# Agent attention with a cosine feed-forward on one core: lots of scores put right behind two kinds of exponential bursts, and the bursts eight steps later

## The chip, the cores and the metric

The kernel runs on one core of one Trainium2 chip. The time is the device time of one execution in microseconds, from a median of three runs. The core has a matrix engine (TensorE, PE in the profile, with its weight loads as PEld), a vector engine (VectorE, DVE), a scalar engine (ScalarE, ACT), GpSimd (POOL) and the engine whose queue starts the transfers (SyncE, SP). Each takes its own instructions in order and waits for the others by semaphores. PE writes only into the banks of PSUM, from which DVE and ACT read.

## The reference

Four batches of 12480 tokens, 128 channels, 49 agents. The agents attend to the keys, the queries attend to the agents, and the result goes token by token through a feed-forward layer with 2048 hidden units and the activation h cos h.

```python
def _attn_ref(q, k, v, agents):
    scale = 1.0 / np.sqrt(q.shape[-1])
    def sm(a, b):
        s = scale * (a @ b.transpose(0, 2, 1))
        s = s - s.max(-1, keepdims=True)
        e = np.exp(s)
        return e / (e.sum(-1, keepdims=True) + 1e-09)
    a2k = sm(agents, k)
    agent_v = a2k @ v
    q2a = sm(q, agents)
    return (q2a @ agent_v).astype(np.float32)

def _moe_ref(x, w_in, w_out):
    h = x @ w_in
    g = h * np.cos(h)
    return (g @ w_out).astype(np.float32)
```

## The kernel before

The tokens of a batch are cut into 13 groups of 960, so there are 52 groups in all. After a prologue, in which the agents of batch 0 are finished and the weights are unpacked, one main loop runs over 832 steps, 16 per group (two halves of 480 tokens, eight pairs of hidden blocks). A step (lines 535 to 572) makes two matmuls of the hidden layer into a double bank `ph` (L543), a sine on ACT (L546, `c`), a product on DVE (L548, `r`), and, four steps later, two matmuls of the output layer into a bank `one` (L565). There are three double banks `ph` and two single banks `one`. One of the two `one` banks holds the sum of the output layer for eight steps; then ACT copies it out (L567, `osb`). So all other uses of `one` share the other bank, one after another.

Between these steps the loop works ahead for later groups and batches. The pieces of this extra work are:

- a **query lot** (`query`, L334 to 351): a tile of 960 queries is loaded (`xt`, three buffers), multiplied with the agents (L92, eight matmuls in the program, sixteen in the trace, into `one`), then DVE takes the maximum of each token (L343, `mx`) and subtracts it (L350, `e`), which sets the bank free;
- a **key lot** (`Agents.scores`, L158 to 182): the same matmuls for 960 keys, then ACT copies the bank out (L171, `s`) and DVE keeps a running maximum (L180 for the first, L182);
- a **burst**: the exponentials of four or five key lots (L214) and of four or five query lots (L354) stand together on ACT, with a table load ahead of and behind them. DVE then sums the query weights and inverts the sums (L358 to 360). Each batch has three bursts, and one earlier burst, of queries 3 to 7, stands at the start of the loop;
- the **maximum** of a batch's keys (`top`, `across`, `spread`) and its subtraction on POOL (L210), which must be over before the first burst;
- the **values** lots (L233), the sums of the exponentials on POOL (L222), and the projection of the new agents into the weights `a` (L264 to 272);
- for each group the weights on POOL (L364) and their transposition (`query_turned`: four matmuls L373, a copy L375 on ACT, casts L378 and L379 on POOL into `pT`).

The places are set by a table of steps made ahead of the loop. `extra` (L451) gives a piece that needs the bank `one` the next free step of those whose place in the run of eight allows it (1, 3, 5; with `dense` 1 to 5). `spread_out` (L464) spreads a list of pieces evenly up to a given step. `BURSTS` (L393) holds the steps of a batch's three bursts, counted from the batch's start. The table fixes in which order the program issues its instructions; the framework then still moves instructions of one engine past each other by estimates of its own, except for the exponentials, which are kept in place. So where a lot's eight matmuls really stand between the `ph` and `one` matmuls is seen only in the built program.

Of the kernel before, what the change touches and what calls it, by code (L numbers as in the profile page):

```python
# [40 lines left out]
def agent_attention_cos_ffn(ctx, tc, qT, kT, v, agT, w_in, w_out, outT):  # L41
    nc = tc.nc
# [108 lines left out]
    class Agents:  # L151
# [3 lines left out]
        def __init__(self, sb, psum, b, wide=None):  # L155
            self.sb, self.psum, self.b, self.wide = sb, psum, b, wide

        def scores(self, g):  # L158
            sb = self.sb
            if g == 0:  # L160
                self.s = sb.tile([TT, NT, NA], F32, name="s", bufs=1)
                self.run = sb.tile([TT, GT, NA], F32, name="run", bufs=1)

                av = sb.tile([P, 2 * HI], F32, name="av", bufs=2)
                self.av, self.sums = av[:, :KR], self.copies(av)
                nc.gpsimd.memset(av[:, NA:HI], 0.0)
                self.es = sb.tile([TT, GT, NA], F32, name="es", bufs=1)
            src = kT[self.b, :, g * GRP:(g + 1) * GRP]
            s = self.part(g)
            if self.wide is None:  # L170
                nc.scalar.copy(s, scores(sb, src, self.b, self.psum()))  # L171
            else:
                if g % 2:
                    xt = sb.tile([P, 2, CH], F32, name="c", bufs=3).rearrange("p j x -> p (j x)")
                else:
                    xt = sb.tile([P, GRP], F32, name="xt", bufs=3)
                ps = scores_twice(xt, src, self.b, self.wide())
                nc.scalar.copy(s.rearrange("p (h t) a -> p h t a", h=2), ps)
            if g == 0:
                nc.vector.tensor_copy(self.run, s)  # L180
            else:
                nc.vector.tensor_max(self.run, self.run, s)  # L182
# [117 lines left out]
    with ExitStack() as pools:  # L300
# [89 lines left out]


        assert NG == 13
        BURSTS = (100, 124, 148)  # L393
        first, early = (0, 1, 2), (3, 4, 5, 6, 7)
        pieces = [tuple(tuple(range(b * NG + x, min(b * NG + y, NQ))) for x, y in ((8, 12), (12, 16), (16, 21))
                        if b * NG + x < NQ) for b in range(NB)]
# [67 lines left out]
        def spread_out(todo, t, end):  # L464

            for i, lot in enumerate(todo):
                t = extra(t, *lot) + 1
                if i + 1 < len(todo):
                    t += max(0, (end - t) // (len(todo) - i - 1) - 1)
            return t  # L470
# [6 lines left out]
        def scored(piece):  # L477
            return [(query, n, piece) for n in piece]

        t = spread_out(scored(early), 0, 0) + 2  # L480
        burst(t, early)
        for b in range(1, NB):
            o, ps = (b - 1) * PER, pieces[b - 1]
            qs, ks = scored(ps[0]), [(ab[b].scores, g) for g in range(NG)]
            if b > 1:
                qs += scored(ps[1])
            both = []
# [10 lines left out]

            for k, at in enumerate(BURSTS):
                at += o  # L500
                for g, n in lots[k:k + 1]:
                    plan(at, pinned_exp, ab[b], g, n)
                burst(at, ps[k])
                for g in range(*((lots[k - 1][0], sum(lots[k - 1])) if k else (0, 0))):
                    plan(at, ab[b].add, g)
                    extra(at, ab[b].values, g, dense=True)
                t = at + (6 if k else 1)
                if k == 0:
                    todo = scored(ps[2]) if b > 1 else scored(ps[1])
                elif k == 1:  # L510
                    todo = [] if b > 1 else scored(ps[2])
                else:
                    todo = []
                    for g in range(lots[2][0], NG):
                        plan(t, ab[b].add, g)
                        t = extra(t, ab[b].values, g) + 2
                t = spread_out(todo, t, o + BURSTS[min(k + 1, 2)] - 4)
# [195 lines left out]
```

## Time and profile before

| what | value |
|---|---|
| median of three runs | 1276.65 us (1271.73 to 1281.36) |
| the profiled execution | 1280.7 us, span 1278.9 us |
| PE busy | 1191.8 us, 93% |
| DVE busy | 1094.8 us, 86% |
| ACT busy | 1029.5 us, 80% |
| POOL busy | 315.2 us, 25% |
| granted PE clock, mean | 0.974 |
| first products (L548) | 83.4 us after the span's start |
| last products | end at 1271.6 us |

The main loop takes 1188 us of the span. A row of a group gives line, engine, operation, tiles and shapes, the number of instructions, then busy time and the mean of one, and the idle time of the engine ahead of them with what ended it. A row of the timeline gives start, length, engine, line, operation, how many were merged, and in brackets the idle time before and what ended it. A row of the windows gives a stretch of time, its length, the busy time of each engine with the number of its instructions, the granted PE clock (1.00 is full speed, 0.50 half) and the share and rate of the transfers.

### The profile page before, as it was taken

How to read it: one execution, taken by the hardware profiler on the slowest of the kernel's cores; microseconds unless marked ns; L12 is line 12 of the kernel's file. 1: busy time of each engine (PE TensorE's matmuls, PEld its weight loads, DVE VectorE, ACT ScalarE, POOL GpSimd, SP SyncE). 2: the span in 40 equal slices, each digit the busy share in tenths (PEclk: the TensorE clock that was granted, in tenths of full speed). 3: DMA queues.
4: the chain of work that ended last, by engine and by line, in shares of the span. 5: the costliest groups of instructions: out<-in, count | busy, mean ns of one | idle time of the engine just before them, and what ended most of it. 6: DMA issues, size and time to landing. Idle time of an engine off the chain costs nothing.

```text
span 1278.9 us, 17272 instructions
## 1 busy us (share of the span) xinstructions
PE 1191.8 (93%) x6349; PEld 961.8 (75%) x6349; DVE 1094.8 (86%) x1217; ACT 1029.5 (80%) x1130; POOL 315.2 (25%) x341
## 2 busy tenths in 40 slices
PE   8998999899999999989999999998999999989997
PEld 8977888687877777768787777777788776667664
DVE  6778888878898888888889888888888999989997
ACT  2357887887798878787979878878888999889997
POOL 1202111621231211162222212224421222121220
PEclk9788999899999999989999999998999999999999
DMA  8762233033412223214231223222320010000000
GB/s 308 223 190 78 77 111 122 32 110 114 135 45 93 77 78 108 78 47 124 78 109 58 66 82 104 77 77 76 95 93 32 31 47 31 16 31 16 32 32 34
DMA packets 39189, 107.74 MB, mean 84 GB/s; under 512 B 4344, under 2 KB 4728, under 8 KB 39096
## 3 DMA queue, kind: packets, MB, share of 16 engines
q1 hardware_dynamic: 39096, 106.55, 26.1%
q8 instruction: 52, 0.85, 0.3%
q14 instruction: 41, 0.34, 0.1%
HBM read 80.97 MB, written 25.56 MB: 83 GB/s over the span
## 4 chain that ended last, share of the span: by engine, by line
PE 57%; DVE 20%; ACT 14%; issue 7%; POOL 1%; DMA 0%; ACTq 0%; SPq 0%; DVEq 0%; POOLq 0%
PE ph L543 20%; DVE r L548 15%; PE one L565 13%; PE one L92 11%; ACT c L546 9%; PE one L233 5%; ACT osb L567 3%; PE ph L233 2%; PE one L561 1%; DVE mx L343 1%; PE one L264 1%; PE ph L100 1%; DVE run L182 1%; PE one L562 1%; ACT e L354 1%
## 5 line engine op out<-in xcount | busy, mean ns | idle before, releaser
L548 DVE SCALAR_TENSOR_TENSOR r<-c,ph 128x960 fp32r<-128x960 f32 x832 | 924.5, 1148 | 108.0 <-ACT c L546 104.1
L546 ACT ACTIVATE c<-ph,half_pi 128x960 f32<-128x960 f32 x832 | 863.2, 1066 | 165.5 <-PE ph L543 145.6
L543 PE MATMUL ph<-pT,a 113*128 113x480 f32 x1664 | 549.6, 411 | 53.9 <-DVE r L548 52.2
L565 PE MATMUL one<-r,w 128*128 128x480 f32 x1664 | 518.0, 391 | 3.8 <-ACT osb L567 3.3
L543 PEld LDWEIGHTS ph<-pT,a 113*128 113x128 f32 x1664 | 285.5, 192 | 178.4 <-DVE r L548 88.5
L565 PEld LDWEIGHTS one<-r,w 128*128 128x128 f32 x1664 | 313.0, 192 | 52.0 <-ACT osb L567 6.4
L364 POOL TENSOR_TENSOR p<-e,rz 120x392 f32<-120x392 f32 x52 | 44.2, 854 | 644.6 <-PE one L373 573.6
L92 PEld LDWEIGHTS one<-ag,xt 128*120 128x120 f32 x1408 | 167.0, 186 | 31.4 <-ACT osb L567 24.1
L92 PE MATMUL one<-ag,xt 128*120 128x49 f32 x1408 | 167.3, 266 | 8.0 <-ACT osb L567 7.0
L379 POOL TENSOR_TENSOR pT<-p,pT 49x480 fp32r<-49x480 f32 x104 | 127.0, 1221 | 7.9
L378 POOL CAST pT<-p 49x480 fp32r<-49x480 f32 x104 | 63.3, 609 | 160.9 <-ACT p L375 156.4
L233 PEld LDWEIGHTS one<-s,vt 120*128 120x128 f32 x624 | 76.5, 191 | 8.2 <-DVE av L238 2.6
L233 PE MATMUL one<-s,vt 120*128 120x98 f32 x624 | 78.2, 273 | 1.1 <-ACT osb L567 0.6
L567 ACT COPY osb<-one 128x480 f32<-128x480 f32 x104 | 57.5, 553 | 2.2 <-PE one L565 2.1
L222 POOL TENSOR_TENSOR es<-es,s 120x392 f32<-120x392 f32 x36 | 36.7, 1019 | 52.3 <-ACT s L214 49.9
L373 PEld LDWEIGHTS one<-ident,p 120*113 120x113 f32 x208 | 30.9, 181 | 16.2 <-ACT osb L567 12.0
L373 PE MATMUL one<-ident,p 120*113 120x120 f32 x208 | 37.4, 279 | 4.4 <-ACT osb L567 3.8
L561 PE MATMUL one<-pT,b 113*128 113x480 f32 x104 | 40.1, 386 | 0.0
L562 PE MATMUL one<-pT,b 113*128 113x480 f32 x104 | 39.7, 382 | 0.0
L375 ACT COPY p<-one 113x480 f32<-113x480 f32 x52 | 28.9, 556 | 12.2 <-PE one L373 12.2
L343 DVE TENSOR_REDUCE mx<-one 120x8 f32<-120x392 f32 x49 | 27.5, 561 | 13.1 <-PE one L92 13.1
L182 DVE TENSOR_TENSOR run<-run,s 120x392 f32<-120x392 f32 x48 | 31.4, 654 | 4.8 <-ACT s L171 2.4
(91 smaller groups left out, 520.3 us busy)
## 6 DMA issues: line engine op xcount, KB each, us to landing
xt<-qT SPq DMA_DIRECT2D x52, 480.0 KB, 3.5
vt<-v SPq DMA_DIRECT2D x104, 240.0 KB, 3.3
outT<-osb SPq DMA_DIRECT2D x51, 480.0 KB, 2.6
xt<-kT SPq DMA_DIRECT2D x46, 480.0 KB, 3.5
c<-kT SPq DMA_DIRECT2D x6, 480.0 KB, 5.9
raw<-w_in SPq DMA_DIRECT2D x8, 256.0 KB, 5.0
raw<-w_out SPq DMA_DIRECT2D x8, 256.0 KB, 4.3
outT<-osb SPq DMA_DIRECT2D x2, 240.0 KB, 2.8
```

The lines of the kernel that those rows point to most:

```text
L92: nc.tensor.matmul(ps[:, t, :], xt[:, t * TT:(t + 1) * TT], ag[:, b, :], start=True, stop=True)
L233: nc.tensor.matmul(po, vt[:, t, :], twice(e[:, t, :]), start=(t == 0 and (g == 0 or not lone)), stop=(t == GT - 1 and (g == NG - 1 or not ...
L373: nc.tensor.transpose(pt[:KR, t * TT:(t + 1) * TT], p_in[n % 2][:, t, :KR], ident[:TT, :TT])
L378: nc.gpsimd.tensor_copy(pT[own, c], p[own])
L379: nc.gpsimd.tensor_sub(pT[other, c], p[own], pT[own, c].bitcast(F32))
L543: nc.tensor.matmul(ph[:, j, :CH], ai[:, f], pTs[q % 3][:, c], start=True, stop=True)
L546: nc.scalar.activation(cos, h, AF.Sin, bias=half_pi, scale=1.0)
L548: nc.vector.scalar_tensor_tensor(r, cos, 1.0, h, op0=ALU.subtract, op1=ALU.mult)
L561: nc.tensor.matmul(po, b1[k], pTs[q % 3][:, c], start=False, stop=False)
L562: nc.tensor.matmul(po, b2[k], pTs[q % 3][:, c], start=False, stop=False)
L565: nc.tensor.matmul(po, w1[:, f, :], r[:, j, :], start=(f == 0), stop=(f == NF - 1))
L567: nc.scalar.copy(osb[:, c * CH:(c + 1) * CH], po)
```

## The change

Three things change in the table of steps, and one in how a key lot is copied.

- The three bursts of each batch stand at steps 108, 132 and 156 of the batch instead of 100, 124 and 148.
- The first three query lots that follow a batch's first burst (queries 12, 13, 14 in batch 1, 29 to 31 in batch 2, 42 to 44 in batch 3) get the next three consecutive steps behind the burst. Before, the first of them got the step behind the burst and the others were spread out.
- The first three key lots of batch 1 get consecutive steps (21, 22, 23) behind the early burst. Before, they stood at steps 21, 29 and 37.
- These three key lots are copied out of PSUM by DVE instead of ACT. All other key lots stay with ACT.

```diff
-        def scores(self, g):
+        def scores(self, g, by_vector=False):
...
-                nc.scalar.copy(s, scores(sb, src, self.b, self.psum()))
+                ps = scores(sb, src, self.b, self.psum())
+                if by_vector:
+                    nc.vector.tensor_copy(s, ps)
+                else:
+                    nc.scalar.copy(s, ps)
...
-        BURSTS = (100, 124, 148)
+        BURSTS = (108, 132, 156)
...
+        def beside(at, todo):
+
+            for lot in todo[:3]:
+                extra(at, *lot, dense=True)
+            return todo[3:]
+
         t = spread_out(scored(early), 0, 0) + 2
         burst(t, early)
+        beside(t, [(ab[1].scores, g, True) for g in range(3)])
+        t += 6
         for b in range(1, NB):
             o, ps = (b - 1) * PER, pieces[b - 1]
-            qs, ks = scored(ps[0]), [(ab[b].scores, g) for g in range(NG)]
+            qs, ks = scored(ps[0]), [(ab[b].scores, g) for g in range(3 if b == 1 else 0, NG)]
...
-                t = at + (6 if k else 1)
+                t = at + 6
                 if k == 0:
-                    todo = scored(ps[2]) if b > 1 else scored(ps[1])
+                    todo = beside(at, scored(ps[2]) if b > 1 else scored(ps[1]))
```

In the changed kernel all lines from 171 on have higher numbers: the hidden layer's matmuls are L555, the sine L558, the product L560, the output layer's matmuls L577, the maximum and the subtraction of a query lot L347 and L354, DVE's copy of a key lot L173.

How the built program's instructions stand is shown at three places. The first is PE at batch 2's first burst (step 308 before, 316 after). Here `ph` is the hidden layer, `r` the output layer, `ag,xt` a lot of scores, `p_94` the transposition of weights. Before, from the last `ph` ahead of the burst's wait on:

```order
L543 MATMUL ph<-pT_89,a_83 128x480 x2
L565 MATMUL one<-r,w_70 128x480 x2
L543 MATMUL ph<-pT_89,a_83 128x480 x2
L565 MATMUL one<-r,w_70 128x480 x2
L373 MATMUL one<-ident,p_94 113x120 x4
L543 MATMUL ph<-pT_89,a_83 128x480 x4
L565 MATMUL one<-r,w_70 128x480 x2
```

The same place after the change:

```order
L555 MATMUL ph<-pT_89,a_83 128x480 x2
L577 MATMUL one<-r,w_70 128x480 x2
L555 MATMUL ph<-pT_89,a_83 128x480 x2
L577 MATMUL one<-r,w_70 128x480 x2
L92 MATMUL one<-ag,xt 120x49 x16
L555 MATMUL ph<-pT_90,a_83 128x480 x2
L577 MATMUL one<-r,w_70 128x480 x2
```

Two whole lots now stand where the four transpositions stood, ahead of the next `ph`.

DVE at the same burst, before; `mx` and `e<-one,mx` are a query lot, `rz` the sums behind the exponentials, `r<-c,ph` the products of the steps:

```order
L548 SCALAR_TENSOR_TENSOR r<-c,ph 128x960 x5
L343 TENSOR_REDUCE mx_4927<-one 120x8
L350 TENSOR_TENSOR e<-one,mx_4927 120x392
L358 TENSOR_REDUCE rz_3577<-e 120x32
L359 TENSOR_SCALAR rz_3577<-rz_3577 120x32
L360 RECIPROCAL rz_3577<-rz_3577 120x32
L548 SCALAR_TENSOR_TENSOR r<-c,ph 128x960 x9
```

And after:

```order
L560 SCALAR_TENSOR_TENSOR r<-c,ph 128x960 x7
L347 TENSOR_REDUCE mx_5015<-one 120x8
L354 TENSOR_TENSOR e<-one,mx_5015 120x392
L347 TENSOR_REDUCE mx_5040<-one 120x8
L362 TENSOR_REDUCE rz_3655<-e 120x32
L354 TENSOR_TENSOR e<-one,mx_5040 120x392
L363 TENSOR_SCALAR rz_3655<-rz_3655 120x32
L560 SCALAR_TENSOR_TENSOR r<-c,ph 128x960
L364 RECIPROCAL rz_3655<-rz_3655 120x32
L560 SCALAR_TENSOR_TENSOR r<-c,ph 128x960 x2
L347 TENSOR_REDUCE mx_5063<-one 120x8
L560 SCALAR_TENSOR_TENSOR r<-c,ph 128x960
```

The second lot's two operations stand around the sums' reduction, and the third lot's behind the third product after the burst.

The third place is PE between the bursts, in batch 2, at the key lot that the table puts at step 225 (b_85 is a part of the projection of the output). Before, all eight of its matmuls stand between the two output matmuls of one step:

```order
L543 MATMUL ph<-pT_90,a_83 128x480 x2
L565 MATMUL one<-r,w_70 128x480
L92 MATMUL one<-ag,xt 120x49 x8
L565 MATMUL one<-r,w_70 128x480
L561 MATMUL one<-pT_89,b_85 128x480
L543 MATMUL ph<-pT_90,a_83 128x480 x2
```

After:

```order
L555 MATMUL ph<-pT_89,a_83 128x480 x2
L577 MATMUL one<-r,w_70 128x480 x2
L92 MATMUL one<-ag,xt 120x49 x3
L555 MATMUL ph<-pT_89,a_83 128x480 x2
L577 MATMUL one<-r,w_70 128x480 x2
L92 MATMUL one<-ag,xt 120x49 x3
L555 MATMUL ph<-pT_90,a_83 128x480 x2
L92 MATMUL one<-ag,xt 120x49 x2
L577 MATMUL one<-r,w_70 128x480 x2
```

The lot is cut into 3, 3 and 2 matmuls over three steps. The other two lots of the sixteen steps stand over two steps each (1 and 7 before, 2 and 6 or 1 and 7 after). At the early burst PE's order is the same up to step 21; two more lots then stand around the second output matmul of step 22, ahead of the `ph` of step 23.

## The prediction

> **What bounds the kernel now.** First the page: one core, 832 steps of the main loop, and three engines that are nearly full.
>
> ```profile
> span 1278.9 us, 17272 instructions
> PE 1191.8 (93%) x6349; PEld 961.8 (75%) x6349; DVE 1094.8 (86%) x1217; ACT 1029.5 (80%) x1130; POOL 315.2 (25%) x341
> ```
>
> No share says what a change is worth; the view by groups gives the parts of a step, and of a lot of scores (a lot is one 960-column tile of q or k).
>
> ```profile
> L548 DVE SCALAR_TENSOR_TENSOR r<-c,ph 128x960 fp32r<-128x960 f32 x832 | 924.5, 1148 | 108.0 <-ACT c L546 104.1
> L546 ACT ACTIVATE c<-ph,half_pi 128x960 f32<-128x960 f32 x832 | 863.2, 1066 | 165.5 <-PE ph L543 145.6 <-DVE r L548 4.3 <-issue 2.3
> ...
> L171 ACT COPY s<-one 120x392 f32<-120x392 f32 x39 | 19.0, 486 | 18.8 <-PE one L92 18.8
> ...
> L180 DVE COPY run<-s 120x392 f32<-120x392 f32 x4 | 1.4, 360 | 1.0 <-ACT s L171 1.0
> ```
>
> Sine and product follow one another at about 1.06 us, so ACT and DVE set a plain step. Where ACT waits, it waits for `ph`, that is for PE. Stretches of the loop show when (windows; columns: length, busy time of PE, PEld, DVE, ACT, POOL, then the granted clock). The first three are 16 steps each by the products (L548) counted in the timeline: one without lots, one with three in batch 2, one with three in batch 1. The last three are the 24 steps from each batch's first burst to its second.
>
> ```profile
> 1162.60:1180.80 18.20, 17.23 (x74) 12.33 (x73) 17.42 (x17) 17.49 (x20) 4.38 (x5) 1.00 0.07 28
> 455.40:478.60 23.20, 21.78 (x123) 17.83 (x122) 19.97 (x22) 18.82 (x22) 4.67 (x5) 1.00 0.27 85
> 156.80:178.90 22.10, 21.21 (x123) 17.98 (x122) 19.60 (x20) 18.79 (x21) 4.44 (x5) 1.00 0.28 91
> 237.70:276.90 39.20, 33.50 (x168) 26.83 (x167) 33.09 (x35) 32.27 (x33) 15.71 (x15) 0.91 0.21 64
> 554.40:595.20 40.80, 34.90 (x185) 29.03 (x183) 33.93 (x37) 32.25 (x34) 15.68 (x15) 0.92 0.25 73
> 863.30:903.30 40.00, 34.07 (x184) 28.39 (x183) 33.83 (x37) 32.10 (x34) 15.70 (x15) 0.91 0.25 75
> ```
>
> A plain step is 18.2/16 = 1.14 us. Three lots add 23.2 - 18.2 = 5.0 us in batch 2 and 3.9 us in batch 1: 1.67 and 1.30 us a lot, because a lot stands in PE's queue ahead of the next `ph`. I use 1.5. With lots the bound is PE, and a lot moved to where PE idles anyway is worth about that. Such a place is the burst; this is the timeline of batch 2's first one.
>
> ```profile
> 554.35 1.28 ACT L214 ACT_TABLE_LOAD   x1
> ...
> 555.43 0.56 DVE L343 TENSOR_REDUCE mx<-one 120x8 f32<-120x392 f32 x1
> 555.64 1.52 ACT L214 ACTIVATE s<-s 120x1568 f32<-120x1568 f32 x1
> ...
> 556.09 0.57 DVE L350 TENSOR_TENSOR e<-one,mx 120x392 f32<-120x392 f32 x1
> ...
> 557.06 1.50 ACT L354 ACTIVATE e<-e 120x1568 f32<-120x1568 f32 x1
> 557.19 0.57 PE L373 MATMUL one<-ident,p 120*113 120x120 f32 x4
> 558.57 1.28 ACT L546 ACT_TABLE_LOAD   x1
> 558.59 1.78 DVE L358 TENSOR_REDUCE rz<-e 120x32 f32<-120x1568 f32 x1 [1.93 <-ACT e L354]
> ...
> 560.41 0.79 DVE L359 TENSOR_SCALAR rz<-rz 120x32 f32<-120x32 f32 x1
> 561.24 0.35 DVE L360 RECIPROCAL rz<-rz 120x32 f32<-120x32 f32 x1
> 561.51 3.22 DVE L548 SCALAR_TENSOR_TENSOR r<-c,ph 128x960 fp32r<-128x960 f32 x3
> ...
> 562.75 2.13 PE L543 MATMUL ph<-pT,a 113*128 113x480 f32 x4 [4.98 <-DVE r L548]
> ...
> 565.48 1.00 PE L543 MATMUL ph<-pT,a 113*128 113x480 f32 x2
> ...
> 567.08 1.00 PE L543 MATMUL ph<-pT,a 113*128 113x480 f32 x2
> ...
> 570.33 1.78 PE L92 MATMUL one<-ag,xt 128*120 128x49 f32 x16
> ```
>
> For 5.5 us ACT makes no sine: table, two exponentials, table. PE fills three `ph` and then idles 4.98 us; DVE idles 1.93 us and then does the sums. PE comes back slow: its `ph` of two consecutive steps, 565.48 and 567.08, lie 1.60 us apart. The last row is the price of a lot on PE, 1.78 us.
>
> **Part by part: the first burst of each batch.** Two more query lots go in here, behind the one that stands ahead of the burst already. Count from the table load (554.35 = 0). The second lot takes PE where the transposes stood, 2.84, for 1.78: 4.62. DVE reduces it (0.56: 5.18), then, by its new order, the sums' reduction (1.78: 6.96, it began at 4.24 before), then subtracts (0.57: 7.53), scales (0.79: 8.3). The first product stands at 8.3; it was 7.16. The third lot waits for the one free bank of `one` until 7.53, ends at 9.3 with a full clock, and only then comes the next `ph`. DVE is the later one: products of three steps and the reciprocal to 11.8, the third lot's reduction 12.4, a product 13.4, its subtraction 14.0. So five steps take 14.0, nineteen plain ones 19 x 1.14 = 21.6, and the lots that stay outside 1.5 each: two in batches 2 and 3, one in batch 1. That makes 38.6, 38.6 and 37.1 against 40.8, 40.0 and 39.2: gains of 2.2, 1.4 and 2.1, mean 1.9. The loads are no limit: `xt` has three buffers, and those of the three lots are free before the burst.
>
> But PE still idles from 4.62 to 7.53, 2.9 us. The rows on the clock, in the windows and the timeline:
>
> ```profile
> 117.90:121.30 3.40, 1.29 (x6) 0.76 (x4) 2.89 (x3) 3.37 (x4) 0.00 (x0) 1.00 0.33 128
> 121.30:128.10 6.80, 6.14 (x17) 5.28 (x18) 5.48 (x7) 5.31 (x7) 4.00 (x5) 0.50 0.00 0
> 561.60:568.40 6.80, 5.65 (x14) 4.42 (x15) 6.13 (x6) 5.08 (x7) 6.51 (x8) 0.50 0.00 1
> ```
>
> ```profile
> 118.38 2.20 DVE L358 TENSOR_REDUCE rz<-e 120x40 f32<-120x1960 f32 x1 [1.43 <-ACT e L354]
> ...
> 121.96 1.17 PE L543 MATMUL ph<-pT,a 113*128 113x480 f32 x2 [2.77 <-DVE r L548]
> ```
>
> At the early burst an idle time of 2.77 us, 2.1 of it inside the 3.4 us before the change, was enough for 6.8 us at 0.50. So I take the half clock as likelier in the new gap too. It costs 0.6 us at the fifth step (the third lot takes 3.6 instead of 1.8, of which DVE's own lateness hides most) and then two steps at the 1.60 above instead of 1.14, about 1.4 together. Forecast per burst: 1.9 - 1.4 = 0.5 gained, 1.5 for three. Bounds: 1.9 each with a full clock; -1.3 each if nothing hides the slow PE (1.8 more for the lot, 1.4 for three steps).
>
> The Trainium skill ("TensorE: Matmul & The Clock Gate", Part 1 on the clock gate) halves the clock only after an idle window of about 3.4 us, and advises against gaps over about 3 us. By that the new gap would keep the full clock and the three bursts would gain 5.7 instead of 1.5. The row of 2.77 us speaks against the rule's letter, so the sum goes by the row.
>
> **The early burst.** One key lot stood behind it already; two more come in, 2 x 1.5 = 3.0. VectorE's copy of a 120x392 tile out of PSUM isn't in the trace: 0.36 us (L180, from SBUF) to 0.57 (L350, from PSUM); I take 0.57, it reads the same place. The first copy and `run` fit into DVE's 1.43 us of idling, the second copy delays the first product by some 0.5, the third stands between products when ACT, three copies of 0.486 lighter, has sines ready. I take 0.4 as lost: 2.6 gained. Bounds: 0 (both lots cost their 1.5 again behind the burst) and 3.5 (the clock stays full too).
>
> **The 8 steps.** Bursts and all that hangs on them (sums, adds on POOL, values, projection, their loads) keep their distances, so most stays equal. What changes is the rhythm of lots in batches 2 and 3: three per 16 steps as before, but key and query change places, and PE's new order cuts one of the three into 3, 3 and 2 over three steps, where it stood whole between two `w` products. Batch 1 has today a stretch with one lot cut that way, and takes 22.1 against 23.2. I take half of that difference, 0.5, for ten stretches (steps 212 to 292 and 420 to 500): 5.0. Bounds: 0 and 10 x 1.05 = 10.5. On POOL the keys' subtractions stand ahead of the casts of the next `pT`:
>
> ```profile
> 549.15 10.48 POOL L210 TENSOR_TENSOR s<-s,mxb 120x1568 f32<-120x1568 f32 x3 [2.99 <-DVE mxb L206]
> ...
> 564.91 1.22 POOL L378 CAST pT<-p 49x480 fp32r<-49x480 f32 x2
> 566.21 2.50 POOL L379 TENSOR_TENSOR pT<-p,pT 49x480 fp32r<-49x480 f32 x2
> ```
>
> After the change they start seven steps ahead of the burst, and that `pT` is first read four steps behind it: 11 x 1.14 + 5.5 = 18 us, for 10.48 and the 1.22 and 2.50 of the casts. I set 0; if POOL were late, each us would cost one per batch.
>
> **Sum:** 2.6 + 1.5 + 5.0 = 9.1 us off the profiled execution's 1280.7 (span 1278.9). The median of the three runs is 1276.65, 4 us less, so 1267.5.
>
> **Rivals.** (1) The clock stays full in the first bursts: 2.6 + 5.7 + 5.0 = 13.3, 1263.3 us. For it: the gap is 40% shorter; whether 2.9 us falls into one stretch of 3.4 or is split over two depends on phase. The rule of the Trainium skill named above gives this case. Against: 2.1 us in one stretch sufficed. Chance 0.2. (2) The cut lots cost as in batch 1: 2.6 + 1.5 + 10.5 = 14.6, 1262 us. For: the cut. Against: batch 1's other lots stand differently. 0.12. (3) Rhythm worth nothing, half clock at full price: 2.6 - 3.9 + 0 = -1.3, 1278 us; the change then does what it says and gains nothing, since lots inside the burst give back on DVE what PE saves. 0.2. (4) Slower: the chain of lots through the one free bank. PE takes instructions in order; the third lot holds back all `ph` until DVE has subtracted the second, which stands behind the sums. If the second lot itself starts late, after the exponentials (4.2 instead of 2.84), PE is idle throughout, both lots run at half clock (3.6 more), and six steps at 1.6 cost 2.8: 6.4 - 1.9 = 4.5 lost per burst, 13.5 in all; the same at the early burst turns 2.6 into -2. With the rhythm worth nothing: 15.5 us, 1292 us. It decides from that start at 4.2 on. Against: the first lot's subtraction ends at 2.31 in the rows, before PE gets there. 0.06. The forecast as summed has the rest, 0.42.
>
> **Numbers.** 1% of this kernel, 12.8 us, is about what a measurement tells from no change. Below 1263.9: rival 2 and two thirds of rival 1, 0.25. Above 1289: 0.06. Between: 0.69. The range runs from 1258 (rivals 1 and 2 in part together) to 1279 (rival 3 and a little); the slower rival and the sum of all upper bounds lie outside.
>
> **What would show it.** In the first bursts two groups of 16 `one<-ag,xt` matmuls between the table load and the fourth sine, PE's gap near 2.9 us instead of 4.98, and a clock of 0.50 behind it or not: that decides rival 1. 24 steps from first to second burst in 37 to 40 us. Behind the early burst three DVE copies L173, and the product of step 25 no later than before, counted from the table load. Sixteen steps of batch 2 near 22.6 us; 23.2 refutes the third term, 22.1 is rival 2. I am wrong if the first product of a burst comes later than about 9 us after the table load, or if a stretch between bursts that I left at zero differs by more than 1 us.

## The result, and the profile after

| | before | after |
|---|---|---|
| median | 1276.65 us | 1264.41 us |
| ratio to before, 95% interval | | 0.9916 (0.9898 to 0.9935) |
| profiled execution | 1280.7 us, span 1278.9 us | 1274.1 us, span 1272.2 us |
| first product after the span's start | 83.4 us | 88.7 us |
| first product to last | 1188.2 us | 1176.4 us |

The medians differ by 12.2 us. The ratio makes the change worth 10.7 us, with an interval of 8.3 to 13.0, a little under 1%; 9.1 were forecast. The profiled execution of after is one of the longer ones: 5.3 us of it lie ahead of the loop. So parts are compared from the first product to the last, where after is 11.8 us shorter. The page of after, and its two groups that stand against those of before:

```profile
span 1272.2 us, 17278 instructions
PE 1190.6 (94%) x6349; PEld 968.3 (76%) x6349; DVE 1092.5 (86%) x1220; ACT 1027.7 (81%) x1127; POOL 312.4 (25%) x341
...
L560 DVE SCALAR_TENSOR_TENSOR r<-c,ph 128x960 fp32r<-128x960 f32 x832 | 926.6, 1148 | 102.7 <-ACT c L558 99.9
L558 ACT ACTIVATE c<-ph,half_pi 128x960 f32<-128x960 f32 x832 | 864.8, 1068 | 167.2 <-PE ph L555 151.3
```

DVE idles 5 us less ahead of its products, but ACT waits for `ph` even longer than before (151 us, before 146). So something new makes `ph` late. The windows show where. In order: 16 steps with three lots in batch 2, then the 24 steps from first to second burst of batches 1, 2 and 3.

```profile
434.28:456.83 22.55, 21.39 (x122) 17.89 (x122) 19.64 (x21) 18.70 (x21) 4.41 (x5) 1.00 0.28 88
248.31:288.31 40.00, 35.32 (x169) 28.22 (x169) 32.41 (x36) 31.75 (x33) 16.82 (x16) 0.91 0.24 74
559.82:602.08 42.26, 37.24 (x192) 30.92 (x192) 33.52 (x39) 31.83 (x33) 16.75 (x16) 0.92 0.26 82
865.38:907.48 42.10, 37.44 (x192) 30.84 (x192) 33.54 (x39) 31.84 (x33) 16.82 (x16) 0.92 0.26 82
```

The 16 steps fell from 23.2 to 22.55 us. The stretches with the three lots got longer, by 0.8, 1.4 and 2.0 us, though lots were moved into the burst to shorten them. The timeline of batch 2's first burst (the table load is at 559.81):

```profile
559.81 1.28 ACT L218 ACT_TABLE_LOAD   x1
...
563.07 1.78 PE L92 MATMUL one<-ag,xt 128*120 128x49 f32 x16
...
565.37 1.78 DVE L362 TENSOR_REDUCE rz<-e 120x32 f32<-120x1568 f32 x1
567.07 0.56 DVE L354 TENSOR_TENSOR e<-one,mx 120x392 f32<-120x392 f32 x1
...
567.72 3.41 PE L92 MATMUL one<-ag,xt 128*120 128x49 f32 x16 [2.87 <-issue]
567.73 1.14 DVE L560 SCALAR_TENSOR_TENSOR r<-c,ph 128x960 fp32r<-128x960 f32 x1
...
570.92 1.15 PE L555 MATMUL ph<-pT,a 113*128 113x480 f32 x2
...
572.10 1.07 ACT L558 ACTIVATE c<-ph,half_pi 128x960 f32<-128x960 f32 x1 [3.81 <-PE ph L555]
...
574.80 1.15 DVE L560 SCALAR_TENSOR_TENSOR r<-c,ph 128x960 fp32r<-128x960 f32 x1
```

PE idles 2.87 us instead of 4.98. Then it runs the third lot at half clock, 3.41 us instead of 1.78, and only behind that lot the `ph` for which ACT has waited 3.81 us.

### The profile page after: what moved, and what is told of

It is laid out like the page before. It is cut to its first block, busy times and chain, and to the rows that moved or that the text cites. A ratio compares the mean times of both kernels' runs of the same rounds, so it can differ in the third digit from the quotient of the medians.

```text
span 1272.2 us, 17278 instructions
## 1 busy us (share of the span) xinstructions
PE 1190.6 (94%) x6349; PEld 968.3 (76%) x6349; DVE 1092.5 (86%) x1220; ACT 1027.7 (81%) x1127; POOL 312.4 (25%) x341
## 4 chain that ended last, share of the span: by engine, by line
PE 60%; DVE 16%; ACT 14%; issue 8%; DMA 1%; ACTq 0%; SPq 0%
PE ph L555 20%; PE one L577 14%; DVE r L560 13%; PE one L92 12%; ACT c L558 10%; PE one L237 4%; ACT osb L579 3%; PE ph L237 3%; PE ph L100 2%; PE one L377 1%; PE one L573 1%; PE one L574 1%; DVE mx L347 1%; DMA xt<-kT 1%; PE one L268 1%
## 5 line engine op out<-in xcount | busy, mean ns | idle before, releaser
L560 DVE SCALAR_TENSOR_TENSOR r<-c,ph 128x960 fp32r<-128x960 f32 x832 | 926.6, 1148 | 102.7 <-ACT c L558 99.9
L558 ACT ACTIVATE c<-ph,half_pi 128x960 f32<-128x960 f32 x832 | 864.8, 1068 | 167.2 <-PE ph L555 151.3
L555 PE MATMUL ph<-pT,a 113*128 113x480 f32 x1664 | 545.7, 408 | 31.3 <-DVE r L560 29.0
L577 PE MATMUL one<-r,w 128*128 128x480 f32 x1664 | 517.6, 391 | 5.0 <-ACT osb L579 4.4
L555 PEld LDWEIGHTS ph<-pT,a 113*128 113x128 f32 x1664 | 285.3, 192 | 145.7 <-DVE r L560 66.9
L577 PEld LDWEIGHTS one<-r,w 128*128 128x128 f32 x1664 | 311.4, 191 | 54.1 <-ACT osb L579 8.4
L92 PEld LDWEIGHTS one<-ag,xt 128*120 128x120 f32 x1408 | 173.8, 189 | 46.4 <-ACT osb L579 28.5
L92 PE MATMUL one<-ag,xt 128*120 128x49 f32 x1408 | 173.9, 269 | 20.5 <-ACT osb L579 11.3
L382 POOL CAST pT<-p 49x480 fp32r<-49x480 f32 x104 | 60.6, 583 | 158.0 <-ACT p L379 154.5
L237 PEld LDWEIGHTS one<-s,vt 120*128 120x128 f32 x624 | 77.5, 191 | 11.0 <-ACT osb L579 4.6
L237 PE MATMUL one<-s,vt 120*128 120x98 f32 x624 | 79.5, 273 | 2.8 <-ACT osb L579 1.6
L226 POOL TENSOR_TENSOR es<-es,s 120x392 f32<-120x392 f32 x36 | 36.7, 1018 | 59.9 <-ACT s L218 57.6
L347 DVE TENSOR_REDUCE mx<-one 120x8 f32<-120x392 f32 x49 | 27.5, 560 | 18.3 <-PE one L92 18.3
L214 POOL TENSOR_TENSOR s<-s,mxb 120x1568 f32<-120x1568 f32 (+1 forms) x9 | 31.6, 3551 | 44.8 <-DVE mxb L210 44.8
L377 PE MATMUL one<-ident,p 120*113 120x120 f32 x208 | 34.4, 275 | 3.4 <-ACT osb L579 3.2
```

What stands on the lines that cost most here:

```text
L92: nc.tensor.matmul(ps[:, t, :], xt[:, t * TT:(t + 1) * TT], ag[:, b, :], start=True, stop=True)
L237: nc.tensor.matmul(po, vt[:, t, :], twice(e[:, t, :]), start=(t == 0 and (g == 0 or not lone)), stop=(t == GT - 1 and (g == NG - 1 or not ...
L377: nc.tensor.transpose(pt[:KR, t * TT:(t + 1) * TT], p_in[n % 2][:, t, :KR], ident[:TT, :TT])
L382: nc.gpsimd.tensor_copy(pT[own, c], p[own])
L555: nc.tensor.matmul(ph[:, j, :CH], ai[:, f], pTs[q % 3][:, c], start=True, stop=True)
L558: nc.scalar.activation(cos, h, AF.Sin, bias=half_pi, scale=1.0)
```

## Experiments

In the table, "loop" is the time from the start of the first product to the end of the last in one profiled execution, "to step 30" the time from the first product to that of step 30, "16" the 16 steps of batch 2, and the last three columns the time from first to second burst of batches 1, 2, 3; all in us, these from the starts of the products in the traces.

| kernel | median | ratio to before | loop | to step 30 | 16 | b1 | b2 | b3 |
|---|---|---|---|---|---|---|---|---|
| before | 1276.65 | | 1188.2 | 52.9 | 23.15 | 39.2 | 40.9 | 40.1 |
| after | 1264.41 | 0.9916 | 1176.4 | 52.3 | 22.55 | 40.0 | 42.3 | 42.1 |
| after, once more | 1264.35 | 0.9917 (0.9885 to 0.9949) | 1174.9 | 51.5 | 22.55 | 40.0 | 42.4 | 40.9 |
| 8 steps alone | 1270.35 | 0.9932 (0.9903 to 0.9961) | 1175.1 | 51.8 | 22.55 | 39.3 | 41.4 | 41.1 |
| early key lots alone | 1273.45 | 0.9965 (0.9938 to 0.9992) | 1185.3 | 52.3 | 23.16 | 39.4 | 40.9 | 40.1 |
| three query lots alone | 1281.14 | 1.0005 (0.9972 to 1.0037) | 1191.0 | 52.9 | 23.15 | 40.4 | 41.7 | 40.9 |
| after, two query lots | 1266.94 | 0.9914 (0.9886 to 0.9942) | 1172.8 | 52.3 | 22.55 | 39.2 | 41.1 | 40.9 |
| the same once more | 1266.76 | 0.9910 (0.9875 to 0.9945) | 1173.2 | 52.2 | 22.55 | 39.5 | 41.2 | 40.9 |
| after, queries as before | 1262.91 | 0.9892 (0.9854 to 0.9930) | 1173.0 | 52.2 | 22.55 | 39.2 | 41.4 | 41.0 |
| sums behind the lots | 1277.49 | 0.9979 (0.9950 to 1.0007) | 1180.8 | 51.0 | 22.55 | 40.9 | 44.9 | 43.8 |
| early lots by ACT | 1278.23 | 0.9992 (0.9964 to 1.0020) | 1185.3 | 59.3 | 22.57 | 39.7 | 43.1 | 42.3 |
| two lots, gap filled | 1258.93 | 0.9845 (0.9798 to 0.9892) | 1167.8 | 51.4 | 22.54 | 37.4 | 39.3 | 39.3 |
| two lots, four fillings | 1267.39 | 0.9902 (0.9866 to 0.9939) | 1175.2 | 52.3 | 22.54 | 39.9 | 41.8 | 41.3 |
| gap filled, the last too | 1255.69 | 0.9820 (0.9775 to 0.9865) | 1165.5 | 50.8 | 22.55 | 37.4 | 39.3 | 39.3 |

Medians of kernels that were run at different times are compared through their ratios, since before had 1276.3 to 1280.8 us beside them. Differences of 2 or 3 us are not resolved in the ratios. The stretches of the loop resolve them: where a stretch holds the same instructions and the same half clock, it repeats from profile to profile within about 0.2 us.

### One part alone: the 8 steps

```diff
-        beside(t, [(ab[1].scores, g, True) for g in range(3)])
-        t += 6
...
-            qs, ks = scored(ps[0]), [(ab[b].scores, g) for g in range(3 if b == 1 else 0, NG)]
+            qs, ks = scored(ps[0]), [(ab[b].scores, g) for g in range(NG)]
...
-                t = at + 6
+                t = at + (6 if k else 1)
...
-                    todo = beside(at, scored(ps[2]) if b > 1 else scored(ps[1]))
+                    todo = scored(ps[2]) if b > 1 else scored(ps[1])
```

> Only the bursts 8 steps on; the query lots and the key lots are placed and copied as before. Theory A (the prediction's sum): the rhythm alone, 5.0 us gained, 16 steps of batches 2 and 3 at about 22.6 us instead of 23.16, and nothing at the bursts. Theory B (the changed kernel's trace: its stretches up to the first bursts of batches 2 and 3 gained 3.7 us each, its stretches from first to second burst lost 0.8, 1.5 and 2.1): the 8 steps carry most of the whole gain, 8 to 11 us, and the stretches from first to second burst lose less than in the changed kernel.

The loop is 13.1 us shorter than before. About 1.2 us of that lie ahead of step 25 (43.7 instead of 44.9), where the clock was low for 6.8 us instead of 10.2, and are not its merit. What is left, 11.9 us, is as much as the whole change gives in the loop (11.8). The other two parts, 2.9 us shorter and 2.8 us longer by the next two sections, nearly cancel. The 16 steps are at 22.55, 0.6 less than before. The stretches with the first bursts got longer by 0.1, 0.5 and 1.0 us: here too PE's built order has a second query lot ahead of the burst's wait in batches 2 and 3, though nothing asks for it.

### One part alone: the early key lots

```diff
-        BURSTS = (108, 132, 156)
+        BURSTS = (100, 124, 148)
...
-                t = at + 6
+                t = at + (6 if k else 1)
...
-                    todo = beside(at, scored(ps[2]) if b > 1 else scored(ps[1]))
+                    todo = scored(ps[2]) if b > 1 else scored(ps[1])
```

> Only the three key lots behind the early burst, copied by VectorE; bursts at 100, 124, 148, queries spread as before. Theories A and B both: 2.6 to 3.5 us gained, all before batch 1's first burst, with 16 steps of batch 2 still at 23.16 us. If the early lots only move the cost, 0 to 1 us.

The loop is 2.9 us shorter, and the part from the first product to the first burst of batch 1 is 3.4 us shorter (150.9 against 154.3); the other stretches repeat those of before within 0.2 us. This term has the forecast sign, and its size is near the upper bound of 3.5, which was that of a full clock. The clock did stay full there. In the three profiles without the early lots (before, the 8 steps alone, the three query lots alone) it was halved for 6.8 us behind the early burst; in the ten with lots copied by DVE it stayed full in eight and was halved for 3.4 us in two. So part of what these lots gain may be that they fill PE's gap; that was not tried by itself.

### One part alone: the three query lots

```diff
-        BURSTS = (108, 132, 156)
+        BURSTS = (100, 124, 148)
...
-        beside(t, [(ab[1].scores, g, True) for g in range(3)])
-        t += 6
...
-            qs, ks = scored(ps[0]), [(ab[b].scores, g) for g in range(3 if b == 1 else 0, NG)]
+            qs, ks = scored(ps[0]), [(ab[b].scores, g) for g in range(NG)]
```

> Only the three query lots in consecutive steps behind each first burst; bursts at 100, 124, 148, key lots as before. Theory A (the prediction's second term): 0.5 us gained per burst, 1.5 in all, the 24 steps from first to second burst at 38.7, 40.3 and 39.5 us. Theory B: 0.8 to 2 us lost per burst, 2 to 6 in all, because the third lot waits in PE's queue and the half clock meets it.

The three stretches are 1.2, 0.8 and 0.8 us longer than before, 2.8 in all, which is the loop's 1191.0 against 1188.2. The forecast said 1.5 us shorter: the sign of this term was wrong, also where nothing else is changed.

### Two lots instead of three, and none

With two lots, for comparison with after on the same chip, and both once more:

```diff
-        def beside(at, todo):
+        def beside(at, todo, many=3):
...
-            for lot in todo[:3]:
+            for lot in todo[:many]:
...
-            return todo[3:]
+            return todo[many:]
...
-                    todo = beside(at, scored(ps[2]) if b > 1 else scored(ps[1]))
+                    todo = beside(at, scored(ps[2]) if b > 1 else scored(ps[1]), 2)
```

> The changed kernel with two query lots behind each first burst instead of three; the third is spread like the rest. Theory A: the third lot costs 1.5 us outside and about 1 inside, so this is 0 to 2 us slower than the changed kernel. Theory B: the third lot is what makes the burst's stretch longer (it holds the next ph back until 7.7 us after the table load and then runs at half clock), so this is 1 to 4 us faster than the changed kernel, and PE resumes with ph, not with a lot.

> The changed kernel itself, beside the next one on the same chip. Its main loop is expected at 1176 us again; what varies from run to run is expected in the part ahead of the loop and in how long the half clock lasts, so the time should go with the mean granted clock: about 1263 us at 0.985 and 1273 at 0.975. If the scatter has another source, time and clock don't go together.

> Two query lots behind each first burst, the third spread: 3 us faster than the changed kernel beside it at the same granted clock (its loop took 1172.8 us against 1176.4). If the two are equal at the same clock, the third lot's place doesn't matter.

And with the queries spread out as before, the other parts kept (`t = at + (6 if k else 1)`, and no `beside` for queries):

> The changed kernel without its first part: the queries are spread out as before, the early key lots and the 8 steps stay. Theory now (three query lots in consecutive steps cost 2.8 to 3.6 us in this kernel, because the third holds back ph at half clock): from the first product to the last 1172 to 1174 us, against 1176.4 and 1174.9 in the two profiles of the changed kernel; first to second burst 39.3, 41.4 and 41.1 us, as in the run of the 8 steps alone. The prediction's own sum (three lots gain 1.5): 1178 us or more. Rival (the lots cost only where the clock was low by chance): within 1 us of 1175. Median: about 1264, not told from the changed kernel.

With two lots the loop takes 1172.8 and 1173.2 us, with the queries as before 1173.0, with three lots 1176.4 and 1174.9. The step from three lots to none shortens the three stretches by 0.9, 0.9 and 1.1 us. So inside the changed kernel, too, the three lots cost about 2.8 us, and two lots neither cost nor gain. In the medians this does not show (0.9892 to 0.9917, intervals overlapping). With the queries as before, though, the built order has a second lot ahead of the burst's wait in batches 2 and 3 all the same, as with the 8 steps alone; so two lots and none differ in batch 1 alone. The timeline of the kernel with two lots at the same burst (table load at 553.85):

```profile
557.11 1.78 PE L92 MATMUL one<-ag,xt 128*120 128x49 f32 x16
...
561.80 1.14 DVE L560 SCALAR_TENSOR_TENSOR r<-c,ph 128x960 fp32r<-128x960 f32 x1
...
563.09 1.14 PE L555 MATMUL ph<-pT,a 113*128 113x480 f32 x2 [4.20 <-DVE r L560]
```

Here PE idles 4.20 us, the clock is halved for 6.8 us as in after, and the first product comes at the same time, 7.95 behind the table load. But the next thing PE makes is `ph`, and not a lot. The fifth product starts 12.8 us behind the table load, in after 15.0.

### Keeping the third lot off the sums

One idea was that the third lot is late since the second one's subtraction stands behind the sums. Here the sums of a first burst are pinned behind the products that the program issues ahead of them.

```diff
-        def query_sums(piece):
+        def query_sums(piece, pin=False):
             rz = rz_of[piece]
-            nc.vector.reduce_sum(rz, e_of[piece], axis=AX.X)
+            ins = nc.vector.reduce_sum(rz, e_of[piece], axis=AX.X)
+            if pin:
+                tc.keep_in_program_order(ins)
...
-                burst(at, ps[k])
+                burst(at, ps[k], k == 0)
```

> The changed kernel, but in the first bursts DVE's sums are held behind the first product, so the three lots follow one another on PE and DVE without the sums between them. Theory C (the half clock is what makes the third lot dear): PE's gap falls from 2.87 to some 1.6 us, the clock stays at 1.00, and the 24 steps from first to second burst take 1.4 us less each than 40.0, 42.3 and 42.1. Theory D (DVE's work is on the path: three lots at 1.13 and the sums at 2.4 have to stand ahead of products anyway): the clock stays full as well, but the first product comes at about 9.2 us after the table load instead of 7.9, and the stretches take the same or up to 1 us more.

It came out unlike either theory: the stretches are 0.9, 2.6 and 1.7 us longer than in after, and the half clock lasts 10.2 to 13.7 us. PE's one gap of 2.87 us became two of 1.31 and 2.41, with the third lot between them. The windows of its batch 2, cut where the clock is set anew:

```profile
561.40:564.80 3.40, 2.09 (x20) 1.96 (x18) 1.13 (x2) 3.37 (x4) 3.19 (x5) 1.00 0.19 25
564.80:568.20 3.40, 3.11 (x16) 2.94 (x16) 0.26 (x1) 2.00 (x3) 3.18 (x4) 0.51 0.33 129
568.20:571.60 3.40, 1.28 (x3) 1.16 (x4) 3.37 (x4) 0.10 (x1) 1.31 (x2) 0.50 0.47 145
```

1.31 us of idling were enough for half clock, in a stretch whose other work was mostly a lot, and a stretch with PE busy for 3.11 of 3.40 us, all of it a lot, did not bring the clock back.

### Who copies the early key lots

```diff
-        beside(t, [(ab[1].scores, g, True) for g in range(3)])
+        beside(t, [(ab[1].scores, g) for g in range(3)])
```

> The changed kernel with the three early key lots copied by ACT like all others. The prediction took DVE's copy at 0.57 us and 0.4 us of it as lost. If VectorE's copies are what lets the early lots hide, the first 30 steps take 52.3 us with them and 53 to 55 with ACT, where three copies of 0.486 us follow the burst's exponentials; if it doesn't matter who copies, within 0.3 us of 52.3.

With ACT copying, step 30 comes 59.3 us behind the first product instead of 52.3, and later than before the change (52.9). ACT is in its exponential when the first key lot is there, so its copy comes behind two sines, and both following lots wait for the bank in turn. They then stand between the `ph`, at half clock, 3.28 us each:

```profile
122.36 0.77 PE L555 MATMUL ph<-pT,a 113*128 113x480 f32 x1 [2.79 <-DVE r L560]
...
122.93 3.28 PE L92 MATMUL one<-ag,xt 128*120 128x49 f32 x16
...
127.34 3.28 PE L92 MATMUL one<-ag,xt 128*120 128x49 f32 x16
```

So the early lots gain because DVE copies them: the bank comes free while ACT is busy. In after the second of the three lots starts 3.6 us behind that burst's table load, in this kernel 7.3.

### Filling the gap

Two lots, and behind the second one PE makes 28 matmuls of 120 columns from constant weights into columns of the bank that the lot leaves free. Nothing reads them.

```diff
+        FILL = 28
...
+                bank = small()
-                ps = scores(sb, src, b, small()).rearrange("p (h t) a -> p h t a", h=2)
+                ps = scores(sb, src, b, bank).rearrange("p (h t) a -> p h t a", h=2)
+                for _ in range(fill):
+                    nc.tensor.matmul(bank[:, GT * NA:], w1[:, 0, :], w1[:, 1, :512 - GT * NA], start=True, stop=True)
...
+            for i, lot in enumerate(todo[:many]):
+                extra(at, *lot, *((False, FILL) if i == 1 and lot[0] is query else ()), dense=True)
...
```

> The kernel with two query lots, and behind the second lot of each batch's first burst PE makes 28 matmuls of 120 columns into unused columns of the same bank; nothing reads them. By the 0.11 us of a lot's matmul they take about 3.1 us, the idle time of 4.20 there. The second lot's maximum then stands behind three products on DVE, so the first product comes 0.5 to 1.1 us earlier than the 7.95 behind the table load. Theory (idle PE brings the half clock, and it costs 1.2 to 1.4 us a burst): clock 1.00 in the first bursts of batches 2 and 3, first to second burst 39.5 to 40.2 us instead of 41.14 and 40.91. Rival (matmuls of few columns don't count as work for the clock: it stayed at 0.50 in windows of 3.4 us that lots filled wholly): half clock of 6.8 us or more, and 41 to 42.5 us, since the filling then also delays ph.

The timeline of its first burst in batch 2 (table load at 552.46), and the window from that burst to the second:

```profile
555.73 1.78 PE L92 MATMUL one<-ag,xt 128*120 128x49 f32 x16
...
557.33 3.32 PE L348 MATMUL one<-w 128*128 128x120 f32 x28
...
559.08 3.28 DVE L564 SCALAR_TENSOR_TENSOR r<-c,ph 128x960 fp32r<-128x960 f32 x3
...
560.48 0.65 PE L559 MATMUL ph<-pT,a 113*128 113x480 f32 x2
```

```profile
552.48:591.77 39.29, 37.65 (x220) 31.16 (x220) 33.44 (x38) 32.20 (x33) 16.82 (x16) 1.00 0.29 89
```

The clock stays at 1.00 and the stretches are 37.4, 39.3 and 39.3 us, 1.9, 1.8 and 1.6 shorter than with two lots alone. This is the first version with lots in the burst whose stretches are shorter than with the queries as before (39.2, 41.4 and 41.0). Whether the lots add anything to what the filling gives was not run: there is no kernel with the filling and without them. The filling also changed DVE's order: the second lot's maximum now stands behind three products, and the first product comes 6.6 us behind the table load. So the order was kept nearly as it is and the filling cut to 4 matmuls (`FILL = 4`):

> As the filled gap, but with 4 matmuls of filling instead of 28 (0.47 us instead of 3.32). DVE keeps the better order: the sums, then the second lot's maximum, and its subtraction behind two products. So PE idles again, from 5.1 to 7.9 us behind the table load by the rows of the filled run, 2.9 us. Theory (the clock is worth most of the filling): half clock of 6.8 us comes back in each first burst of batches 2 and 3, and first to second burst takes 40.3 to 40.9 us, against 39.3 filled and 41.14 and 40.91 with two lots and no filling. Rival (DVE's order was worth it): 39.2 to 39.7 us, with the half clock there and harmless.

The same two views of this kernel (table load at 550.68):

```profile
555.55 0.64 PE L348 MATMUL one<-w 128*128 128x120 f32 x4
...
558.09 1.14 DVE L564 SCALAR_TENSOR_TENSOR r<-c,ph 128x960 fp32r<-128x960 f32 x1
...
559.38 1.14 PE L559 MATMUL ph<-pT,a 113*128 113x480 f32 x2 [3.19 <-DVE r L564]
```

```profile
550.69:592.46 41.77, 37.20 (x196) 30.69 (x196) 34.29 (x39) 32.13 (x33) 16.82 (x16) 0.92 0.27 83
```

PE idles 3.19 us, the clock is halved again, and all the gain is gone, and a little more: 39.9, 41.8 and 41.3 us. The rival (the order was worth it) falls. The first product is 0.8 us later than with the full filling. If that is charged in full, 1.2 to 1.7 of the 2.0 to 2.5 us between the two kernels are left for the slow clock; this is an estimate, since DVE's order still differs around the second lot.

The same at the one burst of the last batch, where PE idled 4.56 us and no lot is near:

```diff
...
+        def filled():
+            bank = small()
+            for _ in range(FILL + 8):
+                nc.tensor.matmul(bank[:, GT * NA:], w1[:, 0, :], w1[:, 1, :512 - GT * NA], start=True, stop=True)
...
             burst(at, piece)
+            if len(piece) > 1:
+                plan(at + 3, filled)
```

> The filled gap, and 36 such matmuls more behind the one burst of the last batch, where PE idled 4.56 us and the clock was at 0.50 for 6.8 us. Theory: clock 1.00 there too, and the stretch behind the last batch's burst 1.2 to 1.9 us shorter, as in the three first bursts; from first to last product 1166 to 1166.6 us against 1167.8. Rival (there DVE's sums, not PE, hold the steps): the clock stays full and the time is within 0.4 us of 1167.8.

The timeline behind the last batch's burst:

```profile
1129.52 3.46 PE L364 MATMUL one<-w 128*128 128x120 f32 x30
...
1134.68 0.67 PE L566 MATMUL ph<-pT,a 113*128 113x480 f32 x2 [1.21 <-DVE r L571]
```

The clock stays full there too, and the time from this burst's product to the last one falls from 119.3 to 117.5 us. No lot was moved here, and the clock was halved for 6.8 us in the one kernel and not in the other, so 1.8 us are the price of that half clock. But 119.3 is the longest that this stretch took. The ten profiles with the bursts eight steps later and no filling here have 118.1 to 119.3 us, all with the clock halved, for 3.4 or 6.8 us of it. Against them the full clock is worth 0.6 to 1.8 us, depending on which steps the half clock meets and for how long. This version takes 0.982 (0.9775 to 0.9865) of before, against 0.9916 (0.9898 to 0.9935) for after: by these intervals it is faster than both kernels.

## Why the prediction came out near

The forecast of 1267.5 is 3 us above the measured 1264.41. It is near by luck: of its three terms one was right, and two were wrong in opposite directions. By the loop (sums of its stretches, before less after; the two that end or begin at a shifted burst with 8 steps of 1.14 us, 9.1 us, taken off or added; the loop's 11.8 above is a difference of rounded times):

| term | forecast | measured |
|---|---|---|
| early burst, up to the first burst of batch 1 | 2.6 | 3.8 (2.9 to 3.4 alone) |
| the three first bursts, first to second | 1.5 | -4.2 |
| all other stretches after the 8 steps | 5.0 | 12.3 |
| sum | 9.1 | 11.9 |

**Early burst: right, at its upper bound.** The three DVE copies are there, at 0.56 or 0.57 us as taken, and hide where I put them; step 25 comes 44.8 us behind the first product, before 44.9. In that execution of after the clock also stayed full there, which is the case of the upper bound of 3.5. With the early lots copied by DVE it did so in eight of ten profiles; the 2.6 had not counted on it.

**First bursts: the sighted steps right, the sum wrong.** The gap (2.9 forecast, 2.87 measured), the half clock behind it in all three batches, the first product (8.3 forecast, 7.92 measured) and the fifth (14.6 with half clock, 15.0 measured) are nearly as I built them. What failed is the step behind that, "nineteen plain ones 19 x 1.14, and the lots that stay outside 1.5 each". With the 0.8 us of its two slow steps it makes 24.0 us from the fifth product to the second burst in batch 1, and 25.5 in batches 2 and 3. Measured were 25.4, 27.3 and 28.1, together 5.9 us more. That is the whole miss of this term, from 1.5 to -4.2; the five steps ahead of it sum to 43.6 us, where I had 43.8.

About 2.1 of it lie in the three steps behind the fifth. One of the lots that stay outside stands whole on PE there:

```profile
577.34 1.78 PE L92 MATMUL one<-ag,xt 128*120 128x49 f32 x16
...
580.75 2.22 DVE L560 SCALAR_TENSOR_TENSOR r<-c,ph 128x960 fp32r<-128x960 f32 x2 [1.86 <-ACT c L558]
```

With this lot and the slow steps, the step makes 5.7 us for these three; they took 6.5, 6.0 and 6.8, in batch 2 at full clock already (the half clock ended at 574.0). DVE waits 1.86 us behind the lot. The other 3.8 us lie in the sixteen steps from the eighth product on, which took 18.9, 21.3 and 21.3 us. In batch 1 no lot is left there, in batches 2 and 3 one, so the step makes 18.2, 19.7 and 19.7. The window of batch 2:

```profile
580.75:602.08 21.33, 19.90 (x102) 15.50 (x101) 19.41 (x21) 17.70 (x20) 4.43 (x5) 1.00 0.19 67
```

The one lot is cut over three steps there, and sixteen matmuls of a values lot (L237) stand there too, ten in batch 1, which I had put at nothing. How the 3.8 us divide among them was not tried.

What a lot that leaves is worth shows against the kernel with the queries as before, which has four more lots behind the fifth products: two in batch 1, one each in batches 2 and 3. Its three stretches from fifth product to second burst sum to 84.8 us, those of after to 80.8. So a lot that leaves saved 1.0 us, not 1.5. The first five steps sum to 36.7 us there and to 43.6 in after. So 6.8 us were lost for 4.0 saved, which is the 2.8 us of the runs above. I priced a lot in the burst only by what it delays on DVE. That it also uses up the `ph` in reserve, so that the next lots cost more, would fit the rows, but no run shows it by itself.

The half clock's 1.4 was not far off where no lot is near it: 0.6 to 1.8 us at the last batch's burst. Beside the lots it seems dearer. The two profiles of after have the same instructions in batch 3; the one had the half clock for 6.8 us there and took 42.1, the other had it for 3.4 and took 40.9, so half of it cost 1.2.

The rest of that term is the shift itself: with the queries as before the three stretches sum to 1.4 us more than before the change, with the three lots to 4.2.

**The 8 steps: size wrong.** The 16 steps came out as forecast (22.6; 22.55), and rival 2, 22.1, did not. But I counted ten such stretches and put the rest at nothing. From 60 steps behind a third burst to the next batch's first burst the time fell by 3.7 us each, 7.3 for the two, not 5.0. Another 5.0 came from stretches that I had left at zero: batch 1's second to third burst 1.6 (43.8 to 42.2), the 60 steps behind each third burst 1.8 together, the tail 1.4, and 0.2 elsewhere. That is the case the prediction named for being wrong, "a stretch that I left at zero differs by more than 1 us". In batch 1 the orders of that stretch before and after hold five lots each and differ in their places; which of these places pays was not tried. That the 16 steps are shorter because a lot is cut into 3, 3 and 2, as I argued, was not tried by itself either.

**The rivals.** (1) The clock stays full: not in the changed kernel, where it was at 0.50 behind each first burst. By the rule of the Trainium skill ("TensorE: Matmul & The Clock Gate", Part 1 on the clock gate), which halves only after an idle window of about 3.4 us, it would have stayed full; the gap of 2.87 us speaks against that figure, as the 2.77 of before did. Its advice against gaps (the same page, "Why this matters for your kernels") was borne out where the gap of 4.20 us was filled. (3) Rhythm worth nothing: refuted by the 16 steps; the other half of it, lots that give back what they save, is what happened. (4) The chain through the one free bank: seen in kind, since the third lot holds `ph` until the second is subtracted, but the second lot started at 3.3, not at 4.2 behind the table load, and the cost was 1 us per burst and not 4.5.

## What to carry to other kernels

Work moved into an idle gap of the matrix engine is not free by itself. Here the lots moved into the three gaps saved 4.0 us further on and lost 6.8 in the first steps, where the engine came back slow and made a lot before the next `ph`. Look at the stretch behind the gap, not only at the gap. Matmuls that nothing reads can be worth more than the lots were: at each first burst 3.3 us of them, with the order of DVE that came along, gave 1.6 to 1.9 us. When a forecast comes out near, compare its terms: two large errors may have met.

## What the runs showed of the hardware

**Half clock followed less idling than I had thought, and lots seem to count less than the records say.** In all fourteen profiles the clock changes only at multiples of 3.41 us. I summed PE's busy time in each such window of the loop at full clock (some 4700) and looked at the clock of the next. 59 were followed by half clock; 57 of these had PE busy 2.26 us or less, and no window below 1.64 us kept the clock. The other two had 3.04 us busy, with lots of scores in them, both at the early burst: of "after, once more" and of "two lots, gap filled". In the first profile of after, the same lots fell otherwise across two windows, and with the same 3.04 us busy the clock stayed full. First the window of "after, once more" and the next one, then, of after, the window with most of the lots:

```profile
113.80:117.20 3.40, 3.03 (x28) 2.73 (x27) 3.37 (x6) 2.99 (x4) 0.22 (x1) 1.00 0.40 102
117.20:120.60 3.40, 3.40 (x10) 2.84 (x10) 3.40 (x5) 1.88 (x2) 0.63 (x1) 0.50 0.58 188
```

```profile
123.46:126.88 3.42, 3.04 (x24) 2.65 (x23) 3.17 (x4) 3.39 (x5) 0.00 (x0) 1.00 0.35 130
```

And a halved clock stayed so while lots ran. With ACT copying the early lots, PE was busy throughout three windows, the first two mostly with lots, before the clock came back at 135.3:

```profile
125.10:128.50 3.40, 3.40 (x16) 3.18 (x15) 1.19 (x2) 1.55 (x2) 0.00 (x0) 0.50 0.33 78
128.50:131.90 3.40, 3.40 (x15) 3.19 (x15) 1.10 (x2) 0.79 (x2) 0.00 (x0) 0.50 0.29 86
131.90:135.30 3.40, 3.40 (x12) 2.96 (x11) 2.31 (x2) 2.26 (x3) 1.60 (x3) 0.50 0.37 128
```

What the clock counts instead of busy time was not settled: the filling, 120 columns behind each weight load, kept it full, and the lots, 49 columns, did not.

**The same program varies by 9 us ahead of the loop.** The two profiles of after, from the start to the first product:

```profile
0.00:88.66 88.66, 78.23 (x553) 74.49 (x553) 61.01 (x126) 29.16 (x49) 11.43 (x25) 0.87 0.77 247
```

```profile
0.00:79.57 79.57, 69.07 (x553) 64.06 (x553) 59.88 (x127) 29.30 (x49) 14.13 (x25) 1.00 0.88 275
```

The instructions are the same; the one had the clock halved for 24 us of this and the other for none. The stretch differs by 9.1 of the 10.6 us by which the spans differ, three quarters of what the whole change gives in the loop. Over the seven executions of "after, once more" the time goes with the mean granted clock: 1262.8 to 1264.4 us at 0.983 to 0.986, 1269.3 to 1271.4 at 0.976 or 0.977. Two profiles must be compared stretch by stretch before a difference of their spans means anything.
